# Batch 0's k softmax through TensorE and a merged weight conversion in an attention and feed-forward kernel

## The chip, the cores and the metric

The kernel runs on one core of one Trainium2 chip. A core has five engines that work in parallel, each through its own queue in order: TensorE (PE in the profile, with its weight loads as PEld), VectorE (DVE), ScalarE (ACT), GpSimd (POOL) and SyncE (SP), which here only issues DMA transfers. The metric is the device time of one execution in microseconds; less is better.

## The reference

Inputs are float32: q, k and v of 8 batches x 8 heads x 576 rows x 64, and two weight matrices of 512 x 2048 and 2048 x 512, which reach the device as 64-bit floats. The computation is a linear attention followed by a feed-forward layer:

```
q_s = softmax of q over its last axis (the 64 columns of a head)
k_s = softmax of k over axis 2 (the 576 rows), column by column
kv  = k_s^T v        (64 x 64 for each batch and head)
att = q_s kv         (576 x 64 for each batch and head)
x   = att, heads side by side: 4608 rows x 512
out = relu(x w_in)^2 w_out
```

The maximum that k's softmax subtracts runs over rows, and rows lie on SBUF partitions. So for k the maximum of a column has to be found across partitions, while q's lies along the free axis of one partition.

## The kernel before

**Stages.** The kernel has a boot stage, in which batch 0's attention is computed, and then nine tiles of the feed-forward layer (t = 0 to 8). Tile t works on batch t's 512 leading rows; the last tile gathers the 64 trailing rows of each batch. While tile t runs its matmuls, the attention of batch t+1 is computed beside it, one pair of heads (p = 0 to 3) in every four steps. A tile has 16 steps f, one for each 128 columns of w_in: `first` (12 matmuls into h), then relu, its square, and `second` (12 matmuls into four accumulators), which runs two steps behind. Matmuls that need float32 accuracy are done as three matmuls on a high and a low part (`wi_h`, `wi_l`, `xh`, `xl` and so on).

**The weights.** The 64-bit weights are turned into float32 on the device, and into high and low parts, once, during boot and tile 0: the other tiles only read them. For each f there is a matrix of w_in ("i") and one of w_out ("o"), 128 x 512 words each. `load_words` (L110) fetches them with SP, `scale_words` (L126) scales the two 32-bit halves of each word on ACT (L130, L131), `join_words` (L133) shifts, masks and adds on DVE (L138, L141, and L146 for "i"), with the addition of "o" on POOL (L148), and `split_words` (L151) makes the high part on ACT (L157) and the low part on POOL (L158). `convert` (L164) works on one matrix a call: it scales the next, joins this one and splits the one before. It is called four times behind boot and twice in each step of tile 0.

**Batch 0's k.** For each pair, `k_max` (L359) reduces the four rows of a partition and takes in the tail rows, `k_turn_max` (L392) transposes that on PE, reduces it along the free axis and spreads the maxima on a diagonal `dg` (L400), `k_shift_pe` (L405) makes of it by a matmul with ones a tile `kmb` that holds the maxima on all partitions, and `k_shift` (L373) subtracts it from k (L377) and from the tail rows (L383) on DVE. `k_exp` (L413) takes exponentials on ACT (L418, L422).

**Buffers.** `pair_tile` puts batch 0's pair 0 in the pool `att`, which later batches use, and pairs 1 to 3 in the pool `boot`, which is closed after boot. So batch 1's first loads go into the buffers that pair 0 has left.

**Order.** Up to the end of tile 0 a scheduler orders each engine's queue by its own estimates of time; from tile 1 on, the queues follow the program text. Within an engine the queue is in order: an instruction that waits holds up all behind it. SP's queue is one such queue for nearly all loads.

Of the kernel before, what the change touches and what calls it, by code (L numbers as in the profile page):

```python
# [22 lines left out]
def attention_ffn(  # L23
# [86 lines left out]
    def load_words(f):  # L110
        pool = const if f < LATE else late
        for name, src in (
            ("i", w_in[:, f * P:(f + 1) * P].rearrange("(kc p) f -> p kc f", p=P)),
            ("o", w_out[f * P:(f + 1) * P, :]),
        ):
# [1 line left out]
            nc.sync.dma_start(
                out=raw if len(src.shape) == 2 else raw.rearrange("p (a b) -> p a b", b=P),
                in_=src,
            )  # L120
# [5 lines left out]
    def scale_words(m):  # L126
        raw = raws[m][2].bitcast
        hi = raw(F32).rearrange("p (n t) -> p n t", t=2)[:, :, 1]
        lo, lo_i = (raw(t).rearrange("p (n t) -> p n t", t=2)[:, :, 0] for t in (U32, I32))
        nc.scalar.mul(out=hi, in_=hi, mul=2.0**-112)  # L130
        nc.scalar.mul(out=lo_i, in_=lo, mul=2.0**-29)  # L131

    def join_words(m):  # L133
        name, f, raw = raws[m]
        lo, hi = (raw.bitcast(I32).rearrange("p (n t) -> p n t", t=2)[:, :, i] for i in range(2))
        w = cvt.tile([P, M], I32, tag="w", name=f"w_{name}{f}")
        ps = bank(f"up_{name}{f}").bitcast(I32)
        nc.vector.tensor_scalar(  # L138
            out=ps, in0=hi, scalar1=3, scalar2=None, op0=ALU.logical_shift_left
        )  # L140
        nc.vector.scalar_tensor_tensor(  # L141
            out=ps if name == "i" else w, in0=hi, scalar=-(2**31), in1=ps,
            op0=ALU.bitwise_and, op1=ALU.bitwise_or,
        )
        if name == "i":
            nc.vector.tensor_tensor(out=w, in0=ps, in1=lo, op=ALU.add)  # L146
        else:
            nc.gpsimd.tensor_tensor(out=w, in0=w, in1=lo, op=ALU.add)  # L148
        raws[m] = (name, f, w.bitcast(F32))

    def split_words(m):  # L151

        name, f, w = raws[m]
# [1 line left out]
        parts = pool.tile([P, 2, M], F32R, tag=f"w{name}{f}", name=f"w{name}{f}")
        hi, lo = parts[:, 0, :], parts[:, 1, :]
        nc.scalar.copy(out=hi, in_=w)  # L157
        nc.gpsimd.tensor_tensor(out=lo, in0=w, in1=hi, op=ALU.subtract)  # L158
        (wi_h if name == "i" else wo_h).append(hi)
        (wi_l if name == "i" else wo_l).append(lo)  # L160
# [33 lines left out]
    def load_kq(b, p, which, queue=nc.sync):  # L194
        t = pair_tile(b, p, [P, 2, C, D], which)
        src = k if which == "k" else q
        queue.dma_start(
            out=t, in_=src[b, 2 * p:2 * p + 2, 0:M, :].rearrange("h (p c) d -> p h c d", c=C)
        )
# [601 lines left out]
```

## Time and profile before

| | us |
|---|---|
| median of 3 runs | 906.83 (906.54 to 906.88) |
| the profiled execution's own time | 908.01 |
| its span, first to last instruction | 906.1 |
| mean granted TensorE clock | 0.992 |

| engine | busy us | share of the span | instructions |
|---|---|---|---|
| PE | 868.4 | 96% | 4028 |
| DVE | 493.5 | 54% | 964 |
| ACT | 347.6 | 38% | 667 |
| POOL | 176.9 | 20% | 214 |

The shares are means over the whole span. The conversion of the weights and batch 0's attention all lie in its first sixth, so what the change touches has to be read there, from tables by stage and from the timeline, where a row gives the start, the duration, the engine, the line of the kernel, the operation, the tile written and the tile read; what stands in brackets is idle time of that engine before the row and what ended it. A busy time of PE is a modelled one and does not mean that PE ran at its peak.

### The profile page before, as it was taken

How to read it: one execution, taken by the hardware profiler on the slowest of the kernel's cores; microseconds unless marked ns; L12 is line 12 of the kernel's file. 1: busy time of each engine (PE TensorE's matmuls, PEld its weight loads, DVE VectorE, ACT ScalarE, POOL GpSimd, SP SyncE). 2: the span in 40 equal slices, each digit the busy share in tenths (PEclk: the TensorE clock that was granted, in tenths of full speed). 3: DMA queues.
4: the chain of work that ended last, by engine and by line, in shares of the span. 5: the costliest groups of instructions: out<-in, count | busy, mean ns of one | idle time of the engine just before them, and what ended most of it. 6: DMA issues, size and time to landing. Idle time of an engine off the chain costs nothing.

```text
span 906.1 us, 11603 instructions
## 1 busy us (share of the span) xinstructions
PE 868.4 (96%) x4028; PEld 721.1 (80%) x4028; DVE 493.5 (54%) x964; ACT 347.6 (38%) x667; POOL 176.9 (20%) x214
## 2 busy tenths in 40 slices
PE   3598998999999999999999999999999999999997
PEld 3477777888888888888888888888888888888886
DVE  7978987555564456555564465545555432233222
ACT  3997444333433334333433343333333422232221
POOL 3375664111111111111111101111111100000000
PEclk9799999999999999999999999999999999999999
DMA  8991112211231122111321131112311020000001
GB/s 236 337 398 45 27 37 70 52 38 38 56 84 38 38 46 81 40 33 36 83 48 38 27 100 39 38 37 56 85 38 38 8 93 1 1 34 15 0 1 47
DMA packets 141194, 57.84 MB, mean 64 GB/s; under 512 B 115920, under 2 KB 134352, under 8 KB 141008
## 3 DMA queue, kind: packets, MB, share of 16 engines
q1 hardware_dynamic: 139424, 55.79, 23.0%
q10 hardware_dynamic: 1712, 1.31, 0.5%
q8 instruction: 32, 0.52, 0.2%
q14 instruction: 26, 0.21, 0.1%
HBM read 46.14 MB, written 10.49 MB: 62 GB/s over the span
## 4 chain that ended last, share of the span: by engine, by line
PE 87%; DVE 5%; ACT 4%; DMA 1%; issue 1%; POOL 1%; SPq 0%; DVEq 0%; ACTq 0%
PE h L549 41%; PE acc L571 40%; PE kv L467 3%; PE x L504 2%; PE kv L470 1%; ACT raw_i L130 1%; DMA kt<-in_k_dram 1%; ACT raw_o L130 1%; ACT raw_o L131 1%; ACT raw_i L131 0%; DVE km L363 0%; POOL w_o L148 0%; ACT r L554 0%; ACT gh L563 0%; DVE w_o L141 0%
## 5 line engine op out<-in xcount | busy, mean ns | idle before, releaser
L549 PE MATMUL h<-xh,wi 128*128 128x512 f32 x1152 | 382.2, 395 | 5.6 <-ACT wi L157 3.8
L571 PE MATMUL acc<-wo,gh 128*128 128x512 f32 x1152 | 348.7, 390 | 4.7 <-ACT gh L563 4.7
L549 PEld LDWEIGHTS h<-xh,wi 128*128 128x128 f32 x1152 | 217.4, 189 | 52.2 <-ACT wi L157 5.1
L571 PEld LDWEIGHTS acc<-wo,gh 128*128 128x128 f32 x1152 | 215.0, 188 | 51.7 <-ACT gh L563 7.6
L549 PE MATMUL h<-xl,wi 128*128 128x512 f32 x576 | 225.9, 392 | 0.2 <-DVE xl L540 0.2
L571 PE MATMUL acc<-wo,gl 128*128 128x512 f32 x576 | 216.4, 389 | 0.0
L555 DVE SCALAR_TENSOR_TENSOR h<-h,r 128x512 f32<-128x512 f32 x144 | 99.6, 692 | 125.7 <-ACT r L554 125.6
L564 DVE TENSOR_TENSOR gl<-h,gh 128x512 fp32r<-128x512 f32 x144 | 99.2, 689 | 114.7 <-ACT gh L563 110.4
L554 ACT ACTIVATE r<-h 128x512 f32<-128x512 f32 x144 | 85.6, 594 | 160.4 <-PE h L549 160.3
L563 ACT ACTIVATE gh<-r 128x512 fp32r<-128x512 f32 x144 | 90.8, 631 | 121.6 <-PE acc L571 120.3
L549 PEld LDWEIGHTS h<-xl,wi 128*128 128x128 f32 x576 | 109.0, 189 | 21.7 <-DVE xl L540 0.5
L571 PEld LDWEIGHTS acc<-wo,gl 128*128 128x128 f32 x576 | 108.0, 188 | 22.4
L377 POOL TENSOR_TENSOR k<-k,kmx 128x512 f32<-128x512 f32 x24 | 30.8, 1284 | 171.3 <-issue 135.7
L389 POOL PARTITION_ALL_REDUCE kmx<-km x24 | 17.4, 726 | 194.5 <-DVE km L367 152.8
L328 POOL TENSOR_TENSOR ql<-qT,qh 128x576 fp32r<-128x576 f32 x24 | 34.2, 1425 | 105.2 <-issue 53.0
L300 ACT ACTIVATE q<-q 128x576 f32<-128x576 f32 x24 | 16.5, 686 | 88.5 <-DVE q L297 79.5
L308 DVE SCALAR_TENSOR_TENSOR bsm<-bsm,sw_s 128x18 f32<-128x18 f32 x24 | 4.5, 189 | 62.0 <-DMA sw_s<-bsm 62.0
L467 PEld LDWEIGHTS kv<-v,ek 128*128 128x128 f32 x256 | 34.5, 197 | 2.4 <-ACT ek L418 0.2
L363 DVE TENSOR_REDUCE km<-k 128x128 f32<-128x512 f32 x32 | 33.9, 1059 | 2.1 <-DMA k<-in_k_dram 2.1
L467 PE MATMUL kv<-v,ek 128*128 128x129 f32 x256 | 35.0, 280 | 0.0
L327 ACT CAST qh<-qT 128x576 fp32r<-128x576 f32 x24 | 16.2, 673 | 42.8 <-DVE qT L320 42.8
L296 DVE TENSOR_TENSOR bmx<-bmx,sw_m 128x18 f32<-128x18 f32 x24 | 4.2, 176 | 46.4 <-DMA sw_m<-bmx 46.4
(93 smaller groups left out, 683.7 us busy)
## 6 DMA issues: line engine op xcount, KB each, us to landing
k<-in_k_dram SPq DMA_DIRECT2D x32, 256.0 KB, 2.8
v<-in_v_dram SPq DMA_DIRECT2D x64, 128.0 KB, 2.9
raw_i<-in_moe_w_in_dram SPq DMA_DIRECT2D x16, 512.0 KB, 7.9
raw_o<-in_moe_w_out_dram SPq DMA_DIRECT2D x16, 512.0 KB, 8.9
out_dram<-o SPq DMA_DIRECT2D x32, 256.0 KB, 2.4
q<-in_q_dram SPq DMA_DIRECT2D x96, 72.0 KB, 2.3
sw_m<-bmx SPq DMA_DIRECT2D x96, 2.2 KB, 1.7
sw_s<-bsm SPq DMA_DIRECT2D x96, 2.2 KB, 1.7
```

The lines of the kernel that those rows point to most:

```text
L130: nc.scalar.mul(out=hi, in_=hi, mul=2.0**-112)
L328: nc.gpsimd.tensor_tensor(out=ql, in0=qt, in1=qh, op=ALU.subtract)
L363: nc.vector.tensor_reduce(out=km.rearrange("p (h d) -> p h d", h=2), in_=kr.rearrange("p h c d -> p h d c"), op=ALU.max, axis=AX.X,)
L377: eng.tensor_tensor(out=kr, in0=kr, in1=kmx.rearrange("p (h d) -> p h d", h=2).unsqueeze(2).broadcast_to([P, 2, C, D]), op=ALU.subtract,)
L467: nc.tensor.matmul(out=ps[:, 0:W], lhsT=kr[:, c, :], rhs=vr[:, c, :], start=(c == 0), stop=False)
L504: nc.tensor.matmul(out=ps[:, 0:SH], lhsT=a, rhs=c[:, cs], start=(j == 0), stop=(j == 2))
L549: nc.tensor.matmul(out=ps, lhsT=w[f][:, p * P:(p + 1) * P], rhs=m, start=(n == 0), stop=(n == 3 * NP - 1))
L554: nc.scalar.activation(out=r, in_=ps, func=AF.Relu)
L555: nc.vector.scalar_tensor_tensor(out=ps, in0=ps, scalar=0.0, in1=r, op0=ALU.max, op1=ALU.mult)
L563: nc.scalar.activation(out=gh, in_=r, func=AF.Square)
L564: nc.vector.tensor_tensor(out=gl, in0=ps, in1=gh, op=ALU.subtract)
L571: nc.tensor.matmul(out=acc[c], lhsT=a[:, cs], rhs=w[f], start=(f == 0 and n == 0), stop=(f == NF - 1 and n == 2),)
```

## The change

For batch 0, k is loaded with the two heads of a row side by side, in runs of 64 numbers. Its maximum is then taken by four transposes of k on PE, whose result is reduced along the free axis from PSUM (`first_max`), with the tail rows' maxima taken the same way for all pairs at once (`first_tail_max`). The shift is no longer a subtraction on DVE: PE adds k, through a matmul with the identity, and the negative maxima, through a matmul of ones with the diagonal `dg`, in one PSUM bank, and ACT takes the exponentials from there (`first_exp`). `dg` is made on ACT. Batches 1 to 7 are computed as before.

The weight conversion now handles the "i" and "o" matrices of a step in one tile: one pair of ACT scalings over 1024 words, one ACT cast of both, and both additions on POOL; `convert` is called twice behind boot and once in a step. Batch 0's pair 3 is placed in `att` instead of pair 0, and batch 0's tail rows of k and q too, so that batch 1's first loads go into the buffers of batch 0's last pair and tail.

```diff
-    cvt = ctx.enter_context(tc.tile_pool(name="cvt", bufs=4))
+    cvt = ctx.enter_context(tc.tile_pool(name="cvt", bufs=2))
...
+    def scale_words(f):
+        hi = part(f, F32, 1)
         nc.scalar.mul(out=hi, in_=hi, mul=2.0**-112)
-        nc.scalar.mul(out=lo_i, in_=lo, mul=2.0**-29)
...
+        nc.scalar.mul(out=part(f, I32, 0), in_=part(f, U32, 0), mul=2.0**-29)
+
+    def join_words(f):
+        lo, hi = part(f, I32, 0), part(f, I32, 1)
+        w = cvt.tile([P, 2, M], I32, tag="w", name=f"w_{f}")
+        for h in range(2):
+            at = slice(h * M, (h + 1) * M)
+            ps = bank(f"up_{f}_{h}").bitcast(I32)
+            nc.vector.tensor_scalar(
+                out=ps, in0=hi[:, at], scalar1=3, scalar2=None, op0=ALU.logical_shift_left
+            )
+            nc.vector.scalar_tensor_tensor(
+                out=w[:, h, :], in0=hi[:, at], scalar=-(2**31), in1=ps,
+                op0=ALU.bitwise_and, op1=ALU.bitwise_or,
+            )
+            nc.gpsimd.tensor_tensor(
+                out=w[:, h, :], in0=w[:, h, :], in1=lo[:, at], op=ALU.add
+            )
...
+        parts = pool.tile([P, 2, 2, M], F32R, tag=f"w{f}", name=f"w{f}")
+        nc.scalar.copy(out=parts[:, :, 0, :], in_=w)
+        for h, (his, los) in enumerate(((wi_h, wi_l), (wo_h, wo_l))):
+            hi, lo = parts[:, h, 0, :], parts[:, h, 1, :]
+            nc.gpsimd.tensor_tensor(out=lo, in0=w[:, h, :], in1=hi, op=ALU.subtract)
...
-        pool = boot if b == 0 and p else att
+        pool = boot if b == 0 and p < NP - 1 else att
...
+        turned = which == "k" and b == 0
+        t = pair_tile(b, p, [P, C, 2, D] if turned else [P, 2, C, D], which)
...
-        t = (att if b else boot).tile(
+        t = att.tile(
             [P, G, D], F32, tag=f"{which}t", name=f"{which}t_{b}", bufs=1
         )
...
+    def first_max(p):
+
+        kr = made["k", 0, p].rearrange("p c h d -> p c (h d)")
+        ps = bank(f"kT_{p}")
+        for c in range(C):
+            nc.tensor.transpose(out=ps[:, c * P:(c + 1) * P], in_=kr[:, c, :], identity=ident)
+        kc = small([P, 1], "kc", f"kc_0_{p}")
+        nc.vector.tensor_reduce(out=kc, in_=ps, op=ALU.max, axis=AX.X)
+        at = p % 2 * 2 + p // 2
+        nc.vector.scalar_tensor_tensor(
+            out=kc, in0=kc, scalar=-1.0, in1=made["ktm"][:, at:at + 1], op0=ALU.mult, op1=ALU.min
+        )
+        dg = small([P, P], "dg", f"dg_0_{p}")
+        nc.scalar.activation(out=dg, in_=ident, func=AF.Copy, scale=kc)
...
+    def first_exp(p):
...
+        nc.tensor.matmul(out=ps, lhsT=ident, rhs=kr, start=True, stop=False)
+        nc.tensor.matmul(
+            out=ps, lhsT=ones, rhs=dg.unsqueeze(1).broadcast_to([P, C, P]), start=False, stop=True
+        )
+        ek = pair_tile(0, p, [P, C, P], "ek")
+        nc.scalar.activation(out=ek.rearrange("p c n -> p (c n)"), in_=ps, func=AF.Exp)
...
-    for _ in range(2 * LW):
+    for _ in range(LW):
         convert()
...
-            if t == 0 and f + LW < NF:
-                convert()
```

The scheduler orders the queues anew. Three places follow; a number behind a name is the tile's serial number.

ACT's queue up to the first cast of a weight, before. The rows `raw_o_384`, `raw_i_386` and `raw_o_388` are scalings of steps 3 and 4, and `xh_3` is the last of batch 0's results that the feed-forward layer needs:

```order
L130 ACTIVATE raw_o_384<-raw_o_384 128x512
L131 ACTIVATE raw_o_384<-raw_o_384 128x512
L511 CAST xh_3_158<-x_3_0_458 128x288
L511 CAST xh_3_158<-x_3_1_464 128x224
L130 ACTIVATE raw_i_386<-raw_i_386 128x512
L131 ACTIVATE raw_i_386<-raw_i_386 128x512
L130 ACTIVATE raw_o_388<-raw_o_388 128x512
L131 ACTIVATE raw_o_388<-raw_o_388 128x512
L157 CAST wi_488<-w_i_476 128x512
```

The same place in the changed queue (`raw_397` is step 3, `w_508` step 0):

```order
L563 CAST xh_3_156<-x_3_0_470 128x288
L563 CAST xh_3_156<-x_3_1_476 128x224
L575 COPY xt_345<-x_2_1_452 128x64
L130 ACTIVATE raw_397<-raw_397 128x1024
L131 ACTIVATE raw_397<-raw_397 128x1024
L156 CAST w_508<-w_488 128x2x512
```

Ahead of the first cast stood the scalings of steps 0 to 4, and now those of steps 0 to 3.

POOL's queue around step 7 of the conversion, before (L148 adds, L158 subtracts):

```order
L148 TENSOR_TENSOR w_o_888<-w_o_888,raw_o_557 128x512
L158 TENSOR_TENSOR wo_923<-w_o_888,wo_923 128x512
L158 TENSOR_TENSOR wi_953<-w_i_918,wi_953 128x512
L148 TENSOR_TENSOR w_o_948<-w_o_948,raw_o_619 128x512
L222 MEMSET v_2_1029 128x4
L158 TENSOR_TENSOR wo_983<-w_o_948,wo_983 128x512
```

The same place in the changed queue (L146 adds, L159 subtracts; `w_888` is step 7, `w_942` step 8, `w_951` the parts of step 7):

```order
L146 TENSOR_TENSOR w_888<-w_888,raw_612 128x512
L278 TENSOR_TENSOR qn_1_838<-q_1_639,sm_1_839 128x2x4x64
L146 TENSOR_TENSOR w_888<-w_888,raw_612 128x512
L146 TENSOR_TENSOR w_942<-w_942,raw_657 128x512
L159 TENSOR_TENSOR w_951<-w_888,w_951 128x512 x2
L146 TENSOR_TENSOR w_942<-w_942,raw_657 128x512
```

A step had three instructions here and has four, and an addition of the next step stands ahead of the subtractions of this one.

SP's queue behind the words of step 1, before (`_364` and up are batch 1's, `raw_i_378` is step 2):

```order
L237 DMA kt_364<-in_k_dram 64x4x64 x2
L237 DMA qt_367<-in_q_dram 64x4x64 x2
L197 DMA k_0_370<-in_k_dram 128x2x256
L197 DMA q_0_372<-in_q_dram 128x2x256
L224 DMA v_0_374<-in_v_dram 128x4x64 x2
L117 DMA raw_i_378<-in_moe_w_in_dram 128x4x128
```

The same place in the changed queue (`raw_394` to `raw_403` are steps 2 to 5):

```order
L238 DMA qt_383<-in_q_dram 64x4x64 x2
L200 DMA k_0_386<-in_k_dram 128x2x256
L200 DMA q_0_388<-in_q_dram 128x2x256
L113 DMA raw_394<-in_moe_w_in_dram 128x4x128
L117 DMA raw_394<-in_moe_w_out_dram 128x512
...
L117 DMA raw_403<-in_moe_w_out_dram 128x512
L247 DMA v_tail<-in_v_dram 64x2x64
L238 DMA kt_380<-in_k_dram 64x4x64 x2
```

Batch 1's tail rows of k, which came ahead of the words of steps 2 to 5, come behind them.

More of the change, by code (lines that the diff above doesn't have):

```diff
@@ L126, in scale_words @@
[L126 to L149, printed above, removed]
@@ L151, in split_words @@
-    def split_words(m):
-        name, f, w = raws[m]
-        pool = const if f < LATE else late
[L155 to L160, printed above, removed]
+        raw = pool.tile([P, 2, M], U64, tag=f"w{f}", name=f"raw_{f}")
@@ L194, in load_kq @@
     def load_kq(b, p, which, queue=nc.sync):
[L195 to L199, printed above, removed]
+        turned = which == "k" and b == 0
+        t = pair_tile(b, p, [P, C, 2, D] if turned else [P, 2, C, D], which)
+        src = (k if which == "k" else q)[b, 2 * p:2 * p + 2, 0:M, :]
+        to = "p c h d" if turned else "p h c d"
+        queue.dma_start(out=t, in_=src.rearrange(f"h (p c) d -> {to}", c=C))
         made[which, b, p] = t
@@ L411, in k_shift_pe, with first_tail_max @@
         k_shift(b, p, ps[:, 0:P], nc.vector)
+    def first_tail_max():
+        ps = bank("ktT")
+        for i in range(2):
+            nc.tensor.transpose(
+                out=ps[:, i * P:(i + 1) * P],
+                in_=made["kt", 0][:, 2 * i:2 * i + 2, :].rearrange("p h d -> p (h d)"),
+                identity=ident,
+            )
+        ktm = small([P, NP], "ktm", "ktm", 1)
+        nc.vector.tensor_reduce(
+            out=ktm, in_=ps[:, 0:2 * P].rearrange("p (n t) -> p n t", t=TL), op=ALU.max, axis=AX.X
+        )
+        nc.vector.tensor_scalar_mul(ktm, ktm, -1.0)
+        made["ktm"] = ktm
+    def first_max(p):
[8 more added lines that the diff above has]
+            out=kc, in0=kc, scalar=-1.0, in1=made["ktm"][:, at:at + 1], op0=ALU.mult, op1=ALU.min
+        )
+        dg = small([P, P], "dg", f"dg_0_{p}")
+        nc.scalar.activation(out=dg, in_=ident, func=AF.Copy, scale=kc)
+        made["dg", 0, p] = dg
+    def first_exp(p):
+        kr = made.pop(("k", 0, p)).rearrange("p c h d -> p (c h d)")
+        dg = made.pop(("dg", 0, p))
+        tl, th = tail_of(0, p)
+        kt = made["kt", 0][:, th, :].rearrange("p h d -> p (h d)")
+        ps = bank(f"ks_0_{p}")
+        nc.tensor.matmul(out=ps, lhsT=ident, rhs=kr, start=True, stop=False)
+        nc.tensor.matmul(
+            out=ps, lhsT=ones, rhs=dg.unsqueeze(1).broadcast_to([P, C, P]), start=False, stop=True
+        )
+        ek = pair_tile(0, p, [P, C, P], "ek")
+        nc.scalar.activation(out=ek.rearrange("p c n -> p (c n)"), in_=ps, func=AF.Exp)
+        ps = bank(f"kts_0_{p}")[:, 0:P]
+        nc.tensor.matmul(out=ps, lhsT=ident, rhs=kt, start=True, stop=False)
+        nc.tensor.matmul(out=ps, lhsT=ones, rhs=dg, start=False, stop=True)
+        nc.scalar.activation(out=kt[tl], in_=ps[tl], func=AF.Exp)
+        made["ek", 0, p] = ek
     def k_exp(b, p):
@@ L576, in store @@
     def store(t, acc, c):
-        o = cvt.tile([P, DM], F32, tag="w", name=f"o_{t}_{c}")
+        if c % 2 == 0:
+            made["o"] = cvt.tile([P, 2, DM], F32, tag="w", name=f"o_{t}_{c}")
+        o = made["o"][:, c % 2, :]
         if t == B and c == C - 1:
@@ L656, in attention_ffn @@
     late = ctx.enter_context(tc.tile_pool(name="late", bufs=1))
-    late.tile([P, 56], F32, tag="pad3", name="pad3")
+    late.tile([P, 48], F32, tag="pad3", name="pad3")
     def prepare(b, p):
```

46 lines of the change are left out of this document (25 added, 21 removed).

## The prediction

> **What bounds the kernel now.** The profile's page comes first: its chain that ended last says which engine sets the end. The table by stage comes next, because the change touches only the first sixth of the span.
>
> ```profile
> PE 87%; DVE 5%; ACT 4%; DMA 1%; issue 1%; POOL 1%; SPq 0%; DVEq 0%; ACTq 0%
> ```
>
> ```profile
> core 0: us, PE busy (x) PEld busy (x) DVE busy (x) ACT busy (x) POOL busy (x), PEclk, DMA share, GB/s
> 0.00:43.75 43.75, 19.68 (x98) 15.29 (x98) 38.40 (x110) 28.02 (x62) 15.25 (x31) 0.90 0.92 282
> 43.75:81.30 37.55, 35.63 (x153) 28.53 (x154) 27.90 (x51) 37.31 (x72) 22.82 (x24) 0.94 0.76 277
> 81.30:148.30 67.00, 62.13 (x292) 50.13 (x291) 59.41 (x108) 31.06 (x59) 43.79 (x41) 1.00 0.13 30
> ...
> 200.00:800.00 600.00, 599.65 (x2804) 501.81 (x2803) 306.69 (x591) 205.31 (x394) 86.27 (x109) 1.00 0.20 46
> ```
>
> I cut the stages at events of the timeline: the first weight matmuls, the step-5 square on ACT, the last relu of tile 0.
>
> ```profile
> 41.98 0.80 PE L549 MATMUL h<-xh,wi 128*128 128x512 f32 x1 [3.27 <-ACT wi L157]
> 42.84 1.28 POOL L158 TENSOR_TENSOR wi<-w_i,wi 128x512 fp32r<-128x512 f32 x1
> 44.08 1.31 POOL L148 TENSOR_TENSOR w_o<-w_o,raw_o 128x512 int32<-128x512 int32 x1
> 80.80 0.68 ACT L563 ACTIVATE gh<-r 128x512 fp32r<-128x512 f32 x1
> 148.29 0.59 ACT L554 ACTIVATE r<-h 128x512 f32<-128x512 f32 x1
> ```
>
> From tile 1 on PE is never idle (599.65 of 600 us), and nothing there is changed, so a microsecond won or lost before 150 us shows in full at the end. Before that there are three stages with three limits. **Boot**, up to about 44 us: DVE works 38.40 of 43.75 us. **Front of tile 0**, to 81 us: ACT works 37.31 of 37.55 us, since its queue scales all 16 steps' words there. **Rest of tile 0**, 67 us: ACT is half idle, PE works 62.13 and DVE 59.41 of it, POOL 43.79. These three feed one another, and 4.9 us of PE are lost.
>
> **Boot, by parts.** DVE's groups of 0 to 43.75 us, and the nearest rows for what is new:
>
> ```profile
> L363 DVE TENSOR_REDUCE km<-k 128x128 f32<-128x512 f32 x5 | 5.2, 1033 | 2.0 <-DMA k<-in_k_dram 2.0
> L264 DVE TENSOR_REDUCE mx<-q 128x8 f32<-128x512 f32 x5 | 3.4, 675 | 0.0
> L377 DVE TENSOR_TENSOR k<-k,kmb 128x512 f32<-128x512 f32 x4 | 2.7, 667 | 0.0
> L367 DVE TENSOR_TENSOR km<-km,kt 64x128 f32<-64x128 f32 x5 | 1.9, 384 | 1.0 <-DMA kt<-in_k_dram 1.0
> L400 DVE TENSOR_SCALAR dg<-ident,kc 128x128 f32<-128x128 f32 x4 | 1.4, 360 | 0.1
> L398 DVE TENSOR_REDUCE kc<-kmT 128x1 f32<-128x128 f32 x5 | 1.4, 286 | 0.7 <-PE kmT L396 0.6
> L383 DVE TENSOR_TENSOR kt<-kt,kmb 64x128 f32<-64x128 f32 x4 | 1.1, 282 | 0.1
> L264 DVE TENSOR_REDUCE mx_t<-qt 128x4 f32<-128x256 f32 x2 | 0.8, 410 | 0.0
> L478 DVE TENSOR_SCALAR ks<-kv 128x1 f32<-128x1 f32 x4 | 0.6, 150 | 0.3 <-PE kv L470 0.3
> ```
>
> Removed for each pair: 1.03 + 0.38 + 0.29 + 0.36 + 0.67 + 0.28 = 3.01 us. Added: a reduction of 512 numbers from PSUM, which the trace lacks; I take 0.68 from L264, and a one-column instruction, 0.15 from L478. That saves 2.18 us a pair and 8.7 us in all, less 0.41 + 0.15 for the tail's maxima: 8.2 us of DVE.
>
> The price stands on PE, in front of the first exponential. A float32 matmul is two records there:
>
> ```profile
> 8.32 0.79 PE L408 MATMUL kmb<-dg,ones 128*128 128x128 f32 x2 [0.78 <-DVE dg L400]
> 10.62 0.63 ACT L418 ACTIVATE ek<-k 128x512 f32<-128x512 f32 x1 [0.60 <-DVE k L377]
> 17.62 1.93 PE L467 MATMUL kv<-v,ek 128*128 128x129 f32 x8
> 26.25 1.06 PE L467 MATMUL kv<-v,ek 128*128 128x129 f32 x8
> ```
>
> Eight records of 129 columns took 1.93 us early and 1.06 later. By columns, 512 in two records cost 1.9 us early (1.05 later). In PE's new queue pair 1's transposes and its product with the identity (about 1.0 + 1.9 + 0.5) stand ahead of pair 0's `dg` product, so the first exponential ends at about 13.3 us where it started at 10.62. I charge 2.7 us, the bound being 0 if DVE has other work meanwhile. At the end of boot the first cast now needs POOL's addition for "i" (1.25 us, the distance of the POOL rows' starts) where DVE's took 0.67 (L146, below), and casts 1024 words (+0.4). Boot: 8.2 - 2.7 - 0.6 - 0.4 = **4.5 us earlier**.
>
> The loads weigh against it. Batch 0's k now lands in runs of 256 bytes, as v always has:
>
> ```profile
> 15.45 0.62 SPq L117 DMA_DIRECT2D raw_i<-in_moe_w_in_dram  x1
> 10.00:15.00 5.00, 0.47 (x1) 0.18 (x1) 5.00 (x13) 2.11 (x5) 2.09 (x2) 1.00 0.72 152
> 40.00:50.00 10.00, 7.95 (x21) 5.62 (x22) 9.74 (x17) 9.76 (x19) 8.42 (x7) 0.57 1.07 387
> ```
>
> From 10 to 15 us, where v moves, the engines made 152 GB/s at a share of 0.72, or 211 GB/s when full; with weights, 387 at 1.07, or 362. Four loads of 256 KB cost 1.24 instead of 0.72 us each: 2.1 us, if all of it shows; k and q are the first loads, and DVE does not run dry of q. I count nothing and keep 2.1 as a bound. [...]
>
> Batch 1's tail k is loaded behind the words of steps 2 to 5. Some 7 MB of words and batch 1's pair 0, from the first words' issue at 15.45 us on, at 362 GB/s put it at 36 to 39 us; DVE wants it at about 41 in its new queue. The cover is 2 us; without it DVE would hold there.
>
> **Front of tile 0.** Here ACT decides, so what boot wins counts only as far as ACT has less to do. The first row shows where the scalings of one kind start and end.
>
> ```profile
> L130 ACT ACTIVATE raw_i<-raw_i x16: 647/686/721, 21.4 to 76.9; 128x512 f32<-128x512 f32 x16
> 53.86 0.66 ACT L130 ACTIVATE raw_i<-raw_i 128x512 f32<-128x512 f32 x1
> 54.41 0.65 ACT L131 ACTIVATE raw_i<-raw_i 128x512 int32<-128x512 uint32 x1
> 54.96 0.62 ACT L418 ACTIVATE ek<-k 128x512 f32<-128x512 f32 x1
> L157 ACT CAST wi<-w_i 128x512 fp32r<-128x512 f32 x16 | 9.9, 617 | 4.7 <-DVE w_i L146 4.7
> L492 ACT CAST kvh<-kv 128x128 fp32r<-128x128 f32 x32 | 9.5, 298 | 39.8 <-DVE kv L482 39.8
> ```
>
> Instructions start 0.56 us apart though each lasts 0.66: they overlap, so merging two saves less than the durations suggest. From 128 to 512 numbers a cast grows by (617 - 298) / 384 = 0.83 ns a number, so 1024 scalings start 0.56 + 0.43 = 0.99 us apart instead of 2 x 0.56. That is 0.13 us for each of 32, 4.2 us, all of it ahead of step 5's square. Six merged casts give 0.5, the four `dg` (0.2 us apart) take 0.8, and the first scaling now waits for both matrices' words (0.3). **3.6 us earlier** at step 5, less than boot's 4.5, so 3.6 counts and boot's remainder is lost in ACT's queue. Bounds: 0 if 1024 cost two times 512, and 4.5, what boot gives.
>
> **Rest of tile 0.** Ten additions leave DVE and go to POOL.
>
> ```profile
> L146 DVE CUSTOM_DVE_ANT_0 w_i<-raw_i,up_i 128x1024 uint16<-128x1024 uint16 x10 | 6.8, 678 | 0.6
> L148 POOL TENSOR_TENSOR w_o<-w_o,raw_o 128x512 int32<-128x512 int32 x10 | 13.2, 1323 | 13.9 <-DVE w_o L141 13.9
> L158 POOL TENSOR_TENSOR wi<-w_i,wi 128x512 fp32r<-128x512 f32 x10 | 12.9, 1290 | 3.5 <-ACT wi L157 3.5
> 136.38 0.50 PE L549 MATMUL h<-xh,wi 128*128 128x512 f32 x1 [0.58 <-ACT wi L157]
> ```
>
> DVE falls from 59.4 to about 52.6 us, POOL rises from 43.8 to 43.8 + 10 x 1.3 = 57 of 67, PE stays at 62.1. PE's idle 4.9 us bounds the gain. POOL mostly waited for DVE's `w_o`, which now comes earlier; but `wi` waits for two additions on the slower engine. I take 2 of the 4.9 us, between the two ends: the limit moves from DVE to POOL, which is nearly as full. **2.0 us.**
>
> **Sum:** 3.6 + 2.0 = 5.6. The profiled execution took 908.01 us, so 902.4 for one like it; the median of the runs shown is 1.2 us lower, so 906.83 - 5.6 = **901.2 us**. The buffers' exchange and the paired output tile I cost at nothing: SP's batch 1 loads hide behind boot, and outputs of tile t wait for stores of tile t-1, some 90 us before.
>
> **The rivals.**
>
> PE unhindered: with DVE relieved, all 4.9 us come back and boot's remainder of 0.9 too. 3.6 + 4.9 + 0.9 = 9.4, 897.4 us. For it: POOL's idle 13.9 us were all spent waiting for DVE. Against: POOL at 57 of 67 us has little room.
>
> No change: 1024 numbers cost ACT two times 512, and POOL's new work eats what DVE saves. 906.8 us. For it: the overlap of neighbours already hides most of an instruction's fixed part. Against: the slope of 0.83 ns.
>
> Slower, one mechanism: the merged conversion waits for its later half. `wi` was ready after DVE's addition, ACT's cast and POOL's subtraction, 0.68 + 0.62 + 1.29 = 2.6 us; now it takes two POOL additions, a longer cast and the subtraction, 2.5 + 1.05 + 1.25 = 4.8 us. The other 2.2 us cost only where the conversion does not lead PE by as much; the row at 136.38 shows PE already waiting for `wi`. If that holds in half of ten steps, 11 us are lost and 3.6 + 3 (half DVE's relief) won: 4.4 us slower, 911.2 us. A second strain adds to it there:
>
> ```profile
> L400 DVE TENSOR_SCALAR dg<-ident,kc x8: 265/367/1358, 8.0 to 138.3; 128x128 f32<-128x128 f32 x8
> L493 DVE TENSOR_TENSOR kvl<-kv,kvh x32: 229/293/951, 24.1 to 716.5; 128x128 fp32r<-128x128 f32 x32
> ```
>
> Small DVE instructions that read and write SBUF stretch from 0.27 to 1.36 us and from 0.23 to 0.95, while POOL works; the large ones, with PSUM on one side, do not. [...]
>
> **Chances.** Forecast 0.46 (its own range 898.5 to 904.5), unhindered 0.22, no change 0.14, slower 0.18. A difference of 0.2%, 1.8 us, is about what a measurement of this kernel can tell. So faster 0.68, same 0.14, slower 0.18. The range runs from 896, PE unhindered and a little more, to 909.5, which leaves out most of the slower case: 0.06 below and 0.13 above.
>
> **What would show it.** Right: the first weight matmul at 37 to 40 us; scalings of 128x1024 starting about 1.0 us apart; step 5's square near 77; DVE at 50 to 54 and POOL at 55 to 58 us between that square and the last relu of tile 0, and that relu at 142 to 144; from there the same rows, shifted. Wrong: scalings 1.1 us apart (no change); PE idle for `w` or for ACT's cast L156 more than five times in tile 0 (slower); PE busy throughout (unhindered); DVE waiting for batch 1's tail k at 41 us; k's first loads holding up the transposes.

## The result, and the profile after

| | before | changed |
|---|---|---|
| median of 5 runs each, us | 906.88 (906.54 to 907.76) | 900.39 (900.03 to 901.97) |
| profiled execution, us | 908.01 | 900.03 |
| its span, us | 906.1 | 898.2 |

The changed kernel takes 0.9929 of the time before (95% interval 0.9915 to 0.9943): 6.5 us less, where 5.6 were predicted. The two profiled spans differ by 7.9 us, 1.4 more than the medians: 908.01 lies above all five times before, and 900.03 is the lowest after. The stages below are of these two executions.

The table by stage, cut at the same events in both (first weight matmul, step 5's square, last relu of tile 0, first relu of tile 1). Its columns are those of the table in the prediction. Before:

```profile
0.00:41.98 41.98, 17.98 (x94) 14.60 (x94) 36.68 (x107) 26.25 (x58) 13.48 (x30) 0.92 0.92 277
41.98:80.80 38.82, 36.83 (x154) 28.79 (x155) 29.12 (x53) 38.58 (x76) 24.32 (x24) 0.91 0.78 287
80.80:148.29 67.49, 62.62 (x294) 50.55 (x293) 59.90 (x109) 31.55 (x60) 44.06 (x41) 1.00 0.12 30
148.29:158.82 10.53, 9.05 (x47) 7.41 (x47) 7.40 (x16) 4.33 (x10) 1.69 (x3) 1.00 0.45 134
```

After:

```profile
0.00:38.05 38.05, 24.79 (x133) 18.53 (x133) 31.24 (x85) 24.91 (x50) 15.77 (x31) 0.88 0.93 281
38.05:78.32 40.27, 36.52 (x160) 28.76 (x161) 31.82 (x57) 38.96 (x51) 32.75 (x32) 0.95 0.83 292
78.32:142.28 63.96, 61.44 (x291) 49.51 (x290) 54.93 (x104) 29.51 (x51) 53.71 (x50) 1.00 0.18 42
142.28:151.25 8.97, 8.97 (x43) 7.55 (x42) 5.12 (x9) 3.53 (x8) 0.90 (x2) 1.00 0.18 56
```

Boot is 3.9 us shorter. The front of tile 0 gives 1.4 of that back (40.27 against 38.82 us), so step 5's square is 2.5 us earlier. The rest of tile 0 is 3.5 us shorter, and the passage to tile 1 another 1.6. At tile 1's first relu the changed kernel leads by 7.6 us, and at the end by 7.9. PE's idle time in the last three stages went from 8.3 us (116.84 less 108.50 busy) to 6.3 (113.20 less 106.93).

The rows that the prediction named, from the timeline after:

```profile
11.31 0.58 ACT L458 ACTIVATE ek<-ks 128x512 f32<-128x512 f32 x1
36.95 1.04 ACT L156 CAST w<-w 128x1024 fp32r<-128x1024 f32 x1 [0.22 <-POOL w L146]
38.05 0.79 PE L601 MATMUL h<-xh,w 128*128 128x512 f32 x1 [4.69 <-ACT w L156]
73.19 1.18 ACT L131 ACTIVATE raw<-raw 128x1024 int32<-128x1024 uint32 x1
74.22 1.18 ACT L130 ACTIVATE raw<-raw 128x1024 f32<-128x1024 f32 x1
75.25 1.16 ACT L131 ACTIVATE raw<-raw 128x1024 int32<-128x1024 uint32 x1
78.32 0.66 ACT L615 ACTIVATE gh<-r 128x512 fp32r<-128x512 f32 x1
142.28 0.60 ACT L606 ACTIVATE r<-h 128x512 f32<-128x512 f32 x1
```

The first weight matmul stands at 38.05 (predicted 37 to 40), scalings start 1.03 us apart (about 1.0), the last of them at 75.25, step 5's square stands at 78.3 (near 77), the last relu at 142.28 (142 to 144). DVE and POOL between the square and that relu show 54.93 and 53.71 us, where 50 to 54 and 55 to 58 were foretold.

What PE waits for from the first weight matmul to tile 1's first relu (total us, times, longest). Before:

```profile
PE acc L571 <- ACT gh L563: 4.7, 6, 1.4
PE h L549 <- ACT wi L157: 3.8, 2, 3.3
PE kmb L408 <- DVE dg L400: 1.4, 1, 1.4
PE h L549 <- ACT xh L539: 1.2, 1, 1.2
```

After:

```profile
PE h L601 <- ACT w L156: 6.8, 3, 4.7
PE kmT L397 <- DVE km L368: 1.2, 1, 1.2
PE acc L623 <- DVE gl L616: 1.0, 1, 1.0
PE h L601 <- POOL w L159: 0.8, 2, 0.6
PE acc L623 <- ACT gh L615: 0.4, 1, 0.4
```

The waits for ACT's square went from 4.7 to 0.4 us. Waits for the converted weights grew, but 4.7 of their 6.8 us lie ahead of the first weight matmul, as 3.3 of the 3.8 did before.

One column of the table by stage was not in the prediction: the granted clock of PE, 0.91 in the front of tile 0 before and 0.95 after. In stretches of half a microsecond it is either 0.50 or 1.00, but for those in which it changes. Before, and then after:

```profile
48.00:48.50 0.50, 0.50 (x2) 0.40 (x2) 0.50 (x1) 0.50 (x2) 0.50 (x1) 0.50 1.01 383
48.50:49.00 0.50, 0.50 (x3) 0.36 (x3) 0.36 (x2) 0.36 (x1) 0.50 (x1) 0.89 1.07 385
```

```profile
41.50:42.00 0.50, 0.50 (x3) 0.40 (x2) 0.50 (x1) 0.50 (x1) 0.50 (x2) 0.50 0.54 86
42.00:42.50 0.50, 0.50 (x2) 0.37 (x2) 0.50 (x2) 0.50 (x2) 0.50 (x1) 0.66 0.82 152
```

From 0.89 and 0.66 the rise is at 48.6 us before and at 42.3 after. So the weight matmuls ran at half clock for 6.6 us before and 4.3 after. In the kernel before, three of them take 1.28 us at 0.50 (46.05 to 47.33, from start to start) and 0.68 at 1.00 (49.54 to 50.22), so about half of such time is lost: an estimated 3.3 and 2.1 us. By this estimate 1.2 us of what was won comes from the clock, and no step of the prediction spoke of it. In the runs that kept PE busy, further on, the clock rose earlier (at 37.9 and 40.7 us instead of 42.3), and PE idled longer behind it (7.4 and 8.6 us instead of 6.3).

### The profile page after: what moved, and what is told of

Same layout as the page of the kernel before. It is cut to its first block, busy times and chain, and to the rows that moved or that the text cites. A ratio compares the mean times of both kernels' runs of the same rounds, so it can differ in the third digit from the quotient of the medians.

```text
span 898.2 us, 11645 instructions
## 1 busy us (share of the span) xinstructions
PE 873.6 (97%) x4066; PEld 724.2 (81%) x4066; DVE 483.9 (54%) x934; ACT 343.1 (38%) x623; POOL 196.1 (22%) x230
## 4 chain that ended last, share of the span: by engine, by line
PE 86%; DVE 4%; ACT 3%; DMA 3%; issue 2%; POOL 1%; SPq 1%; DVEq 0%; POOLq 0%; ACTq 0%
PE acc L623 40%; PE h L601 40%; PE kv L519 2%; PE x L556 2%; DMA raw<-in_moe_w_out_dram 1%; ACT raw L131 1%; DVE up L139 1%; ACT raw L130 1%; DVE w L142 1%; PE kv L522 1%; POOL w L146 1%; DMA k<-in_k_dram 0%; SPq L225 0%; DVE h L607 0%; DMA sw_m<-bmx 0%
## 5 line engine op out<-in xcount | busy, mean ns | idle before, releaser
L601 PE MATMUL h<-xh,w 128*128 128x512 f32 x1152 | 381.5, 395 | 7.7 <-ACT w L156 6.8
L623 PE MATMUL acc<-w,gh 128*128 128x512 f32 x1152 | 348.4, 390 | 0.6 <-ACT gh L615 0.4
L601 PEld LDWEIGHTS h<-xh,w 128*128 128x128 f32 x1152 | 216.7, 189 | 54.6 <-ACT w L156 7.6
L623 PEld LDWEIGHTS acc<-w,gh 128*128 128x128 f32 x1152 | 215.4, 188 | 46.1 <-ACT gh L615 1.9
L601 PE MATMUL h<-xl,w 128*128 128x512 f32 x576 | 225.5, 392 | 0.0
L623 PE MATMUL acc<-w,gl 128*128 128x512 f32 x576 | 216.9, 390 | 1.0 <-DVE gl L616 1.0
L623 PEld LDWEIGHTS acc<-w,gl 128*128 128x128 f32 x576 | 108.0, 188 | 23.7 <-DVE gl L616 1.3
L601 PEld LDWEIGHTS h<-xl,w 128*128 128x128 f32 x576 | 108.7, 189 | 20.9
L146 POOL TENSOR_TENSOR w<-w,raw 128x512 int32<-128x512 int32 x32 | 41.5, 1315 | 6.3 <-DVE w L142 5.5
L159 POOL TENSOR_TENSOR w<-w,w 128x512 fp32r<-128x512 f32 x32 | 40.8, 1301 | 8.6 <-ACT w L156 8.5
```

What stands on the lines that cost most here:

```text
L146: nc.gpsimd.tensor_tensor(out=w[:, h, :], in0=w[:, h, :], in1=lo[:, at], op=ALU.add)
L159: nc.gpsimd.tensor_tensor(out=lo, in0=w[:, h, :], in1=hi, op=ALU.subtract)
L601: nc.tensor.matmul(out=ps, lhsT=w[f][:, p * P:(p + 1) * P], rhs=m, start=(n == 0), stop=(n == 3 * NP - 1))
L623: nc.tensor.matmul(out=acc[c], lhsT=a[:, cs], rhs=w[f], start=(f == 0 and n == 0), stop=(f == NF - 1 and n == 2),)
```

## The experiments

Times are medians of 4 to 12 executions; ratios are to the kernel before on the same chip, whose medians there were 907.1 to 907.7 us. The changed kernel's 900.39 us stands against 906.88 before, so differences of less than 1 us from it are read from the ratios.

**Batch 0's k alone, and the merged conversion alone.** Each half of the change on the kernel before, with the old buffers. The first puts the three new functions in the place of `k_max`, `k_turn_max`, `k_shift_pe` and `k_exp`:

```diff
-        k_max(0, p)
+            first_tail_max()
+        first_max(p)
...
-        k_shift_pe(0, p)
-        k_exp(0, p)
+        first_exp(p)
```

The second scales, joins and splits both matrices of a step at once, as the changed kernel does:

```diff
-    for _ in range(2 * LW):
+    for _ in range(LW):
         convert()
...
-    late.tile([P, 56], F32, tag="pad3", name="pad3")
+    late.tile([P, 48], F32, tag="pad3", name="pad3")
```

> The kernel before with batch 0's k through TensorE (turned load, maxima from PSUM, shift by matmul, dg on ScalarE), the old conversion and the old buffers. Theory: boot gets some 4 us shorter, so the first weight matmul comes 3 to 4 us earlier (38 to 39 us), but ScalarE's scalings set the front of tile 0, so step 5's square comes at most 1 us earlier than 80.8 us and the rest of tile 0 keeps its length of 67 us: 905.5 to 906.9 us. Rival (what boot wins is kept to the end): 902 to 903.5 us.

> The changed kernel with batch 0's k and the buffers as before, so the merged conversion alone. Theory: the conversion holds most of the gain: step 5's square some 2 us earlier, the rest of tile 0 three to four us shorter than 67 us: 901 to 903 us. Rival (the merged conversion waits for its later half and only pays with the shorter boot): 905.5 to 908 us.

k alone took 908.37 us, 1.0016 of before (1.0008 to 1.0025); the conversion alone 906.28, 0.9996 (0.9981 to 1.0012). Neither gained. The second time lies where that run's rival had it, but by luck: the reason was another. In both runs tile 1's first relu came 3.7 and 6.6 us earlier than before (155.07 and 152.23 against 158.82). What was won there got lost later: nearly every tile from the second on took 95.57 and 95.54 us, where before and changed kernel take 95.04, with PE never idle. The relus (ACT) of steps 8 and 12 of one tile and of step 0 of the next show where, with k alone:

```profile
580.09 0.60 ACT L605 ACTIVATE r<-h 128x512 f32<-128x512 f32 x1 [1.82 <-PE h L600]
603.88 0.60 ACT L605 ACTIVATE r<-h 128x512 f32<-128x512 f32 x1 [1.85 <-PE h L600]
633.59 0.60 ACT L605 ACTIVATE r<-h 128x512 f32<-128x512 f32 x1 [2.17 <-PE h L600]
```

Four steps take 23.79 us, and the next four, with what ends the tile, 29.71. The weights of steps 12 to 15 lie in a pool of their own, which begins behind the filler `pad3`. In the changed kernel the new small tile `ktm` and the narrower filler offset each other; with one of them alone the pool is shifted by a few bytes in each partition against the two kernels.

**The same two with the late weights back in their place.** Only the filler's width is changed, from 56 to 48 numbers and from 48 to 56.

> Batch 0's k on TensorE alone, as in the run of that name, but with the filler ahead of the late weights' pool 48 instead of 56 numbers wide, so that these weights lie 32 bytes lower, where the kernel before and the changed kernel have them. Placement theory: the half microsecond that each tile from 1 on took longer goes away, tiles of 95.04 us instead of 95.57, and the time falls by 4.5 to 5 us, to about 903.7 (903 to 904.5). Rival (the longer tiles come from something else in the k path, such as loads or ScalarE): tiles stay at 95.5 us and the time at 907.5 to 909.

> The merged conversion alone, as in the run of that name, with the filler 56 instead of 48 numbers wide, so that the late weights lie where the kernel before and the changed kernel have them. Placement theory: tiles of 95.04 us instead of 95.54, and 901.6 us (900.8 to 902.5) instead of 906.3. Rival: 905.5 to 907, tiles as long as they were.

k alone now took 903.12 us, 0.9956 (0.9943 to 0.9968), and the conversion alone 901.22, 0.9932 (0.992 to 0.9945): 5.2 and 5.1 us less for 32 bytes. The same relus of the first:

```profile
576.33 0.60 ACT L605 ACTIVATE r<-h 128x512 f32<-128x512 f32 x1 [1.82 <-PE h L600]
600.09 0.60 ACT L605 ACTIVATE r<-h 128x512 f32<-128x512 f32 x1 [1.82 <-PE h L600]
629.29 0.60 ACT L605 ACTIVATE r<-h 128x512 f32<-128x512 f32 x1 [2.13 <-PE h L600]
```

The four steps take 23.76 us, nearly as in the run before (23.79), and what follows 29.20 instead of 29.71. So only the matmuls of the late weights had been slower, 0.5 us a tile for 96 of them, 5 ns each: there the starts of matmuls lie 232 ns apart in that run and 227 in this one, by the median. Placement is shown to be the cause; by what path the 32 bytes slow a matmul is not.

**The exchange of buffers: left out, alone, and with the merged conversion.**

```diff
-        pool = boot if b == 0 and p < NP - 1 else att
+        pool = boot if b == 0 and p else att
...
-        t = att.tile(
+        t = (att if b else boot).tile(
```

This is the changed kernel without it; the other two runs make the opposite edit, in the kernel before and in that with the merged conversion in its place.

> The changed kernel with batch 0's pair 0, not pair 3, in the shared buffers and with its tail rows of k and q in the boot pool, as before. Theory: these loads hide behind boot, the time stays within 0.7 us of 900.4. Rival (the words of steps 2 to 5 come earlier because batch 1's tail k and v stand behind them in SP's queue, and that is part of the gain): 901.5 to 904 us.

> The kernel before with only batch 0's last pair and tail placed where its pair 0 was, so that batch 1's first loads wait for the last pair. Theory by the prediction's step (the exchange by itself is worth nothing, and counts only where the conversion is shorter than the loads it hides): 906 to 907.7. Rival (the words of steps 2 to 5 come ahead of batch 1's loads and that alone is worth what the changed kernel lost without the exchange): first weight matmul 2 us earlier and 902.5 to 904.5.

> The merged conversion (901.2 us with its late weights in place) with the buffers' exchange, and batch 0's k as before. Theory (the exchange pays wherever the conversion is the merged one, since then words and scalings decide): 1 to 4 us less, 897 to 900.3. Rival (the exchange costs 4 us with the old k, as it did on the kernel before, and only k's new path, which frees VectorE early, turns that round): 903 to 906. Same time within 0.9: the exchange matters for k's path alone.

Without it the changed kernel took 904.43 us, 0.9968 (0.9956 to 0.998), 4 us more. Alone it made the kernel before slower, 911.05 us, 1.0046 (1.0033 to 1.0059). Both expectations of that run missed. With the merged conversion it took 904.49, 0.9969 (0.9959 to 0.9979), as the rival had it, where the conversion without it took 901.22. So the exchange is worth -4 us in one setting and +4 and +3 in two others. In the changed kernel it lets SP issue the words of step 2 ahead of batch 1's v. The issue of these words without the exchange, and then with it:

```profile
27.41 0.70 SPq L113 DMA_DIRECT2D raw<-in_moe_w_in_dram  x1
```

```profile
21.86 0.97 SPq L113 DMA_DIRECT2D raw<-in_moe_w_in_dram  x1
22.96 0.76 SPq L117 DMA_DIRECT2D raw<-in_moe_w_out_dram  x1
```

Without it, ACT also stands still ahead of the scalings: batch 1's q waits in its queue for POOL.

```profile
33.88 0.63 ACT L481 ACTIVATE q<-q 128x512 f32<-128x512 f32 x1 [2.08 <-POOL q L266]
...
34.94 1.14 ACT L130 ACTIVATE raw<-raw 128x1024 f32<-128x1024 f32 x1
```

The first weight matmul comes 2.3 us later (40.32), the clock rises at 48.6 instead of 42.3, and a second spell at half clock follows a wait of PE. The mean granted clock of all five executions points the same way: 0.988 to 0.989, and 0.990 to 0.991 in the five of the changed kernel.

```profile
88.30 2.68 PE L623 MATMUL acc<-w,gh 128*128 128x512 f32 x8 [1.94 <-ACT gh L615]
90.00:93.00 3.00, 3.00 (x14) 2.81 (x13) 2.78 (x5) 0.00 (x0) 3.00 (x4) 0.50 0.03 8
```

With the exchange alone, such a spell comes too:

```profile
90.52 2.06 PE L467 MATMUL kv<-v,ek 128*128 128x129 f32 x8 [2.66 <-ACT wi L157]
91.00:93.00 2.00, 2.00 (x11) 2.00 (x10) 1.97 (x3) 1.14 (x2) 2.00 (x3) 0.50 0.00 0
```

There PE idles 11.5 us up to tile 1's first relu instead of 8.3. Earlier words alone do not explain the gain: with the exchange alone and with the merged conversion, SP issued the words of step 2 at 19.96 and 19.00 us, where they stood at 26.58 in the kernel before and at 26.12 with the conversion alone, and both runs lost. What in the queue's order makes the old k or the old conversion lose by the exchange is not settled.

**Additions of w_in back on DVE.**

```diff
-                out=w[:, h, :], in0=hi[:, at], scalar=-(2**31), in1=ps,
+                out=w[:, h, :] if h else ps, in0=hi[:, at], scalar=-(2**31), in1=ps,
...
+            if h:
-            nc.gpsimd.tensor_tensor(
+                nc.gpsimd.tensor_tensor(
...
+            else:
+                nc.vector.tensor_tensor(out=w[:, h, :], in0=ps, in1=lo[:, at], op=ALU.add)
```

> The changed kernel with the addition of the w_in matrix back on VectorE. Theory: VectorE was the fullest feeder of the rest of tile 0, so it is busy about 60 us there again and the time is 902 to 904 us. Rival (the additions on GpSimd cost as much as they save, since the cast of both halves waits for two of them): 899 to 900.6 us.

907.27 us, 0.9999 of before (0.999 to 1.0008): the whole gain is gone, twice what was expected of this part. The rest of tile 0:

```profile
77.97:151.12 73.15, 66.07 (x306) 51.95 (x306) 61.29 (x117) 30.43 (x51) 44.33 (x42) 1.00 0.15 37
```

With DVE at 61.29 and POOL at 44.33 us, as before the change, that stage takes 73.15 us instead of 63.96, though step 5's square stands at 77.97 as in the changed kernel. PE idles 7.1 us there (2.5 in the changed kernel); the other 4.6 us are more work of PE inside the stage (66.07 against 61.44 us busy), of which a shorter passage to tile 1 gives part back. This agrees with the prediction's cause, the relief of DVE. But the run moves queue places as well as additions: its first weight matmul also comes 1.5 us later, and half clock costs 1.5 more by the estimate above. So its whole size isn't a price of the additions, and the relief is not shown by itself.

**ScalarE's instructions cut in two again.**

```diff
-        nc.scalar.mul(out=hi, in_=hi, mul=2.0**-112)
-        nc.scalar.mul(out=part(f, I32, 0), in_=part(f, U32, 0), mul=2.0**-29)
+        for h in range(2):
+            at = slice(h * M, (h + 1) * M)
+            nc.scalar.mul(out=hi[:, at], in_=hi[:, at], mul=2.0**-112)
+            nc.scalar.mul(out=part(f, I32, 0)[:, at], in_=part(f, U32, 0)[:, at], mul=2.0**-29)
...
-        nc.scalar.copy(out=parts[:, :, 0, :], in_=w)
+            nc.scalar.copy(out=parts[:, h, 0, :], in_=w[:, h, :])
```

> The changed kernel with ScalarE's scalings and casts of a step cut into two of 512 numbers again, all else as changed. Theory (the merging on ScalarE is what moves step 5's square, 32 pairs of 0.56 us against 32 of 1.03, 2.9 us, and six casts, 0.5): the square of step 5 about 3 us later than in the changed kernel, near 81.5, and the time 902.5 to 904. Rival (the square's place came from boot, and ScalarE only followed): the square within 1 us of 78.3 and the time within 0.8 of 900.4.

903.55 us, 0.996 (0.9946 to 0.9974): 3.2 us more than the changed kernel, as the theory had it. The place was another.

```profile
77.69 3.68 PE L625 MATMUL acc<-w,gh 128*128 128x512 f32 x8 [2.25 <-ACT gh L617]
78.06 0.72 ACT L133 ACTIVATE raw<-raw 128x512 int32<-128x512 uint32 x1
78.00:81.00 3.00, 3.00 (x8) 2.32 (x8) 3.00 (x6) 3.00 (x7) 1.65 (x3) 0.50 0.00 0
79.64 0.66 ACT L617 ACTIVATE gh<-r 128x512 fp32r<-128x512 f32 x1
```

The last scaling starts at 78.06, 2.8 us later than in the changed kernel (75.25), about the 2.9 of the spacing (32 x (2 x 0.56 - 1.03)). Step 5's square came only 1.3 us later. By the three numbers further on, 1.5 us come from a later first weight matmul and an estimated 3.3 from the clock, less 0.8 of idle time: a wait of 2.25 us with half clock behind it, and the first rise at 47.0 instead of 42.3. So the time agrees with the spacing's price without being shown to come from it.

**Keeping PE busy ahead of the first weight matmul.** Seventeen, and then ten, matmuls whose results are thrown away are put into the bank of `h` ahead of the first real one:

```diff
+        made["keep"] = (kvl, ql)
...
         ps = ps_h.tile([P, M], F32, tag="h", name=f"h_{t}_{f}")
+        for _ in range(17 if t == 0 and f == 0 else 0):
+            kvl, ql = made["keep"]
+            nc.tensor.matmul(out=ps, lhsT=kvl, rhs=ql[:, 0:M], start=True, stop=True)
```

> The changed kernel with 17 matmuls of 512 columns added ahead of the first weight matmul, whose results are thrown away: they fill the 4.7 us in which TensorE there waits for the first cast. In the traces so far the granted clock falls to half between 28 and 35 us, in spells of 3.4 us or a multiple, and stays there until 42 to 49 us. Theory (the idle time ahead of the first weight matmul keeps the clock down, and costs the changed kernel half of the 4.3 us between that matmul and the clock's rise, 2.1 us): the clock is full at the first weight matmul or at most 1 us later, and the time 897.5 to 899.5. Rival (the clock has its own reasons, or what it gives is taken up by waits for ScalarE's casts): the clock rises at 42 us as before, or it rises and the time stays within 0.8 of 900.4.

> As the run that kept TensorE busy ahead of the first weight matmul, with 10 matmuls instead of 17: those 17 ended at 40.5 us, 1.6 us after the first cast, and a second spell at half clock came at 79 us. Theory (shorter filling keeps the early rise of the clock and gives the 1.6 us back): first weight matmul at 38.5 to 39.3, its clock full within 1 us, and 897.5 to 899.8. Rival (what the clock gives at 40 us is lost again in waits for the conversion further on): the clock up as well, and 900 to 901.8.

With 17, PE at the first weight matmul, and the clock:

```profile
35.00 5.49 PE L600 MATMUL h<-ql,kvl 128*128 128x512 f32 x17 [0.97 <-ACT xt L576]
40.33 0.40 PE L605 MATMUL h<-xh,w 128*128 128x512 f32 x1
38.50:60.00 21.50, 19.46 (x93) 15.72 (x92) 17.29 (x33) 19.99 (x26) 20.67 (x18) 1.00 0.96 343
```

The clock is full from 37.9 us on; in the changed kernel, where the 4.7 us are idle, it rose at 42.3. The first half of the theory holds. The time is 901.18 us (0.993, 0.9916 to 0.9944), not better than the changed kernel's, as the rival had it. The first weight matmul started 1.65 us after the first cast had ended (38.68), and a second spell at half clock came at 78.85 us. With ten the clock rose at 40.7 us and the first weight matmul started at 39.06, but the time was 904.3 us (0.9964, 0.9951 to 0.9976): PE idled 8.6 us up to tile 1's first relu instead of 6.3, with a spell at 95 us. The rival of that run has the direction, what the clock gives at 40 us is lost further on, but the time lies above its 901.8. Both runs also changed the order of the other queues further on, so the filling is not their only difference.

**The order of the program text in tile 0.** The scheduler is switched off from tile 0 on, and three steps are converted ahead:

```diff
-    LW = 2
+    LW = 3
...
-        if t == 1:
+        if t == 0:
             ctx.enter_context(tc.manual_schedule())
```

> The changed kernel with the queues of tile 0 in the order of the program text, as the later tiles have them, and three steps converted ahead instead of two. Theory (of the 6.3 us that TensorE idles between the first weight matmul and tile 1's first relu, most comes from the order that the scheduler chose): idle time of 3 us or less there and 894 to 898.5. Rival (it comes from how far the conversion leads TensorE, whatever the order): idle time as long or longer, 900 to 906, with the first weight matmul later than 38 us because a third step is converted ahead of it.

927.93 us, 1.0226 (1.0207 to 1.0245). PE idles 22.7 us up to tile 1's first relu (137.49 less 114.79 busy), most of it for DVE:

```profile
PE kmT L397 <- DVE w L142: 12.3, 4, 3.6
PE kmb L409 <- DVE w L142: 3.7, 1, 3.7
```

Both theories were too mild. The program's order and the longer lead together cost 27.5 us against the changed kernel: by the three numbers below 16.4 us of idle time, an estimated 9.6 of half clock and 1.0 from the later first weight matmul. They weren't run apart.

**The runs by three numbers.** All with the late weights in place (most tiles take 95.04 us). Worked out from each run's profile: where its first weight matmul starts, PE's idle time from there to tile 1's first relu, and half of the time at half clock in that stretch, the estimate of its price from above.

| run | first weight matmul | idle | half clock costs | sum | time |
|---|---|---|---|---|---|
| before | 42.0 | 8.3 | 3.3 | 53.6 | 906.9 |
| changed | 38.1 | 6.3 | 2.1 | 46.5 | 900.4 |
| k alone, in place | 40.8 | 5.1 | 2.1 | 48.0 | 903.1 |
| conversion alone, in place | 39.7 | 5.6 | 3.2 | 48.5 | 901.2 |
| 17 kept busy | 40.3 | 7.4 | 1.7 | 49.4 | 901.2 |
| 10 kept busy | 39.1 | 8.6 | 2.5 | 50.2 | 904.3 |
| ScalarE cut in two | 39.6 | 5.5 | 5.4 | 50.5 | 903.6 |
| without the exchange | 40.3 | 4.8 | 5.9 | 51.0 | 904.4 |
| conversion and exchange | 40.8 | 7.6 | 2.8 | 51.2 | 904.5 |
| w_in added on DVE | 39.5 | 8.4 | 3.7 | 51.6 | 907.3 |
| exchange alone | 40.4 | 11.5 | 4.5 | 56.4 | 911.1 |
| order of the text | 39.0 | 22.7 | 11.7 | 73.4 | 927.9 |

Time less sum lies between 851.8 and 855.7 us, so these three carry most of what the runs differ by. They come from the profiled execution of each run; its span less the sum lies between 850.5 and 853.2 us in all twelve. This is bookkeeping: it says where the time went, and not why. What remains may be work of batch 1 that the queues put ahead of that relu or behind it; it wasn't traced.

## Why the prediction was right, and where it was not

The time was right, 900.4 against 901.2, and so was the frame: what is won before 150 us shows at the end, and three stages feed one another. The terms were right in their signs, and less so in size and cause.

**Boot, 4.5 us; measured 3.9.** The price on PE was mis-sized: the first exponential ended at 11.89 us instead of 13.3, and started at 11.31, 0.7 later than before and not 2.7. Of the 2.7, 0.6 came from setting the new one's end against the old one's start. Most of the rest is PE's pace: the step charged pair 1's product with the identity at the early 1.9 us, which pair 0's took, but pair 1's took 1.02:

```profile
5.82 1.92 PE L453 MATMUL ks<-k,ident 128*128 128x512 f32 x2
9.06 1.02 PE L453 MATMUL ks<-k,ident 128*128 128x512 f32 x2
```

The trace's records of the granted clock begin, at full, at 8.21 us in the changed kernel, where PE has work from 4.94 us on, and at 21.31 us before. Half clock until then is an estimate: 1.92 is 1.88 times 1.02 us, as 1.28 is of 0.68 above. No record shows it. By the step's own terms boot should now have won 6.5 us. It did not, and the step that failed is "8.2 us of DVE" as a gain of boot: k alone, in place, starts its weight matmuls only 1.2 us earlier (40.82), the merged conversion, which this step charged with 1.0, 2.3 us earlier (39.66). Up to the first weight matmul DVE worked 5.4 us less (31.24 against 36.68), not 8.2, and its idle time grew from 5.3 to 6.8 us, so its work alone did not set boot's end. What did is open.

**The loads, counted at nothing.** From 3 to 8 us, where k and q move, the engines made 250 GB/s at a share of 1.09, where they had made 288 at 0.97: 229 and 297 GB/s when full. The first words were issued at 16.81 us, where they had been at 15.45; in all runs with the new layout they were issued at 16.28 to 17.01 us, in all with the old one at 15.15 to 16.12. So some of the 2.1 us may have shown. The direction agrees with the prediction's two rates, 211 GB/s where v moves and 362 with weights. The price of the new layout is open, since it was not tried by itself.

**Front of tile 0, 3.6 us; measured 2.5 at the square.** The spacing of 0.99 us was 1.03, which makes 2.9 of 4.2. The first scaling, charged with 0.3 us for waiting on the words of both matrices, started 1.8 us later (23.14 against 21.35). The last one stood here before:

```profile
79.15 0.71 ACT L131 ACTIVATE raw_o<-raw_o 128x512 int32<-128x512 uint32 x1
```

At 75.25 us it is now 3.9 us earlier, as much as the first weight matmul, so boot's remainder was not lost in ACT's queue; the square lost part of it.

**Rest of tile 0, 2.0 us; measured 3.5, of which 2.4 are idle time of PE.** The step was meant as idle time of PE, and of the 4.9 us 2.4 came back, so its size was nearly right. The other 1.2 us of the stage are work of PE that now lies outside it (61.44 us busy against 62.62). The cause given, the relief of DVE, agrees with the run that put the additions back, where the stage takes 73.15 us, but that run moved queue places too. The 1.6 us of the passage to tile 1 were in no step. There PE had waited 1.2 us for `xh`; in the changed kernel it is busy for all of its 8.97 us.

**The buffers' exchange, nothing; measured 4 us.** This step failed outright. In SP's queue, the third piece of order in the section on the change, the words of steps 2 to 5 come ahead of batch 1's tail rows. The prediction read it as a danger for these rows, not as a gain for the words. By the three numbers, leaving the exchange out costs 2.3 us at the first weight matmul and an estimated 3.7 of half clock, and wins 1.5 of idle time. That the earlier words bring this is argued, and not shown, since in two other settings they came earlier still and the exchange lost. The danger did not arise: the row of `km` shows no wait for a load, only a long duration while POOL works, from 43.09 us on (0.28 us at 11.30 in the kernel before).

```profile
43.34 1.18 DVE L368 TENSOR_TENSOR km<-km,kt 64x128 f32<-64x128 f32 x1
```

**Not in the prediction at all:** the half clock (1.2 us of the gain, by the estimate above), and the filler. That its width went from 56 to 48 was in the full diff only as a number; had it stayed, the changed kernel's late weights would lie as in the run with k alone, and by the two runs with k alone that is worth an estimated 5 us.

**The parts do not add up.** k gives -4.0, the conversion -5.9, both without the exchange -2.8 and with it -6.5. So it is in part luck that a sum of parts came within 1 us: three omissions partly cancel, parts that spoil one another's order of the queues, the exchange that mends it, and the clock. The total was predicted rightly, but the working that led to it is borne out only for the idle time that came back in the rest of tile 0 and, nearly in size, for the spacing of ACT's scalings.

**The rivals.** The slower one set PE idle for the converted weights more than five times; it was five, 7.6 us with the 4.7 ahead of the first weight matmul. The unhindered one needed all of PE's idle time in the rest of tile 0, and half came back. The one of no change needed scalings 1.1 us apart, and they stand 1.03 apart.

## What to carry to other kernels

Before pricing a change in a scheduled kernel, look at every queue that it reorders, loads above all, and treat the parts as one: two parts that each win 4 to 6 us may win 3 together. Read the granted clock in short stretches wherever PE waits for about 2 us or more, since behind nine of thirteen such waits here, of 1.86 to 3.66 us, the clock was 0.50 for the next 3.4 us or more, which by the estimate above costs about half of that time besides. When an experiment adds or drops a tile, keep the placement of what lies behind it, or the comparison measures the placement (5 us here).

## What the runs showed of the hardware

**Half clock.** After stretches in which PE was often idle (busy for 0.53 of the 3.41 us up to the fall at 34.96 us in the kernel before, and for 1.79 of those up to the fall at 28.69 in the changed kernel) the granted clock was 0.50, in spells of 13.7 us (before and changed, around the end of boot), 17.1 (without the exchange, there too) or 3.4 (behind single waits): 4, 5 and 1 times 3.41 us. The spells lie on a fixed grid: in each of the fourteen traces all changes of the clock are whole multiples of 3.413 us apart. In the kernel before, the rise at 48.61 us and the last fall, at 905.36 by this row, are 251 of them apart.

```profile
905.00:905.50 0.50, 0.00 (x0) 0.00 (x0) 0.00 (x0) 0.00 (x0) 0.00 (x0) 0.86 0.00 0
```

From 42 us on the traces have thirteen waits of PE of 1.86 to 3.66 us. Nine, in six runs, were followed by such a spell; four, of 2.04, 2.06, 2.13 and 2.90 us, were not. Cut along the grid, PE was busy for 0.07 to 0.43 of the stretch ahead of each of the nine spells, while each of the other four waits lay across two stretches that were both busy for 0.43 or more. So in these traces the fall went with a wait's place on the grid, and not with its length alone. A threshold isn't shown: the busy time is modelled, and near the end of boot the clock also fell behind a stretch that was busy for 0.64, at 31.78 us in the run in the order of the text.

**Placement of weights.** With k alone, moving the weights of four steps by 32 bytes in each partition made their matmuls some 5 ns slower, 232 instead of 227 ns from start to start, 5 us for the kernel (908.37 against 903.12), with PE busy throughout; no wait or idle time shows it.
